# A hand-listed order for attention through inducing points and a SwiGLU network on one core, listed anew

## The chip, the cores and the metric

One core of a Trainium2 chip runs the whole program. The metric is device time in microseconds (us), the median of the runs shown. TensorE (PE in the profile), VectorE (DVE), ScalarE (ACT) and GpSimd (POOL) each work through their own queue in order and wait for one another by semaphores. SyncE (SP) issues nearly all DMAs. TensorE has two rows in the profile: PE is the matmuls, PEld the loads of stationary weights ahead of them.

## What is computed

Four batches of 12416 rows with 128 channels go through two attention steps (32 learned rows look at the input, then the input looks at the 32 rows that come out), and every row of the result goes through a gated network of 1536 hidden channels behind an RMS norm.

```python
def mab(q, kv):                      # B, N, C = 4, 12416, 128; inducing has 32 rows
    s = scale * (q @ kv.transpose(0, 2, 1))
    s = s - s.max(-1, keepdims=True)
    a = np.exp(s)
    a /= a.sum(-1, keepdims=True) + 1e-09
    return a @ kv
h = mab(I, x)
x = mab(x, h)
...
xn = x / np.sqrt(np.mean(x * x, axis=-1, keepdims=True) + 1e-06) * rms_g
g = xn @ w_gate                      # 128 -> 1536
silu = g * (1.0 / (1.0 + np.exp(-g)))
out = silu * (xn @ w_val) @ w_out    # 1536 -> 128
```

## The kernel before

**Tiling.** The rows of a batch are cut into 25 units: 20 of 512 columns, 4 of 480 and one of 256. A unit meets the 1536 hidden channels in 12 chunks of 128, so the network has 4 x 25 x 12 = 1200 blocks. Attention's second step is folded into the gate and value weights (the stacks "sg" and "sv"), so a block starts from the attention weights "a" of its unit.

**A block.** It takes a gate product (`gate`, L656) on TensorE, its SiLU on ScalarE (`silu`, L666), a value product on TensorE (`value`, L684) and their product on VectorE (`times_value`, L698). The way from there to the output is one of three kinds, a letter for each block in the string `sorts`:

- P, plain: one matmul with 32-bit weights (`project_plain`; it appears at L754 with the weight "wo", as two records).
- S, split: a rounded upper half on ScalarE (`high`, L711), the rest on VectorE (`low`, L717), two matmuls with rounded weights (`project_two`, L742 and L743), the sum of both halves on GpSimd (`add_in_place`, L762), and a third matmul (`project_third`, also L754, with weights from "xn" or "more").
- D, split as well: the upper half on ScalarE (`high`, L708), the rest on GpSimd (`low_of_u`, L724), one more step on ScalarE (`high_down`, L730), and then as S from `project_two` on.

So an S block costs VectorE one step more than P, GpSimd one, ScalarE one, and TensorE three short matmuls in place of the plain one. A D block costs GpSimd two steps and ScalarE two more than P.

**The end of a unit.** `scale_up` (L786, ScalarE), `finish` (L795, VectorE), `turn_out` (L801, VectorE) and `store` (L814, four DMAs).

**Attention for the next batch** runs among the blocks of the one before: 1132 small steps ("micros"), among them loads (L100, L111), transposes of the input (L301), scores (L318), sums (L370), and for each set of units a chain that makes the norm (L523 to L582). `gather` (L594) copies the result of that chain into the tile "a" of a unit by four DMAs.

**The order.** Up to the first gate product the order is a list of names (`ORDER`). Everything behind it is a string: `program` (L1257) has a letter for each step, "." being the next of the micros, whose number is in `taken` (L1361). The steps are issued in the order of the letters, and since every engine runs its queue in order, the string fixes the order on all engines and on SP's DMA queue. Six more strings go with it: `banks` (L1141) names the PSUM bank, of eight, that each matmul group writes, `workers` (L1168), `outputs` and `holders` (L1175) name buffers in SBUF, `sorts` (L1198) has the kinds, and `picks` (L1211) says which of the blocks that are ready a step takes. A matmul into a bank waits until the last reader of what the bank held before is done; for a gate product's bank that is `silu`, for a value product's bank `times_value` or, with S blocks, `low`.

```python
do = {"g": gate, "s": silu, "y": lambda: silu(True), "x": gate_times, "v": value, "m": times_value, "h": high, "l": low,
      "n": low_of_u, "e": high_down, "q": project_two, "d": add_in_place,
      "r": project_third, "p": project_plain, "E": scale_up, "F": finish, "T": turn_out, "O": store, "a": lambda: gather(*next(gathered))}
for name in "".join(program.split()):
    if name == ".":
        step, args = micros[int(next(taken))]
        step(*args)
    else:
        do[name]()
```

Of the kernel before, what the change touches and what calls it, by code (L numbers as in the profile page):

```python
# [23 lines left out]
def kernel(  # L24
# [1100 lines left out]
    def seams():  # L1125
# [16 lines left out]
        0234567120374516023741053614753614753641734617543671543613565436125461234512351364127153421432415304251034521342  # L1142
        1546243612631246347631475236423426407234673427637542374532052315034150432015245371453741037637167351675062701231
        7517017374534130142042301270432174126436741562174327156714506134614561056035462013663276261651762307157643054603
        1405364051342605341643625672174251670517614057427645705460760370274261462347347634627475617543206750135401657154
        7014605726415240657465364025423743043045012751350537056175017136731653725702170516751745246754275271263417345325
        0123102431042106524623603240546037426340731037610371057615763516370535610357413713527412534127302503243410145125
        6154572450125062012576173563057037143603607360246327407207320734263121450214352142451320461204321323131435714357
        1437513265615063105607157105612703106302610427640736273073042562364235463253462536712467126512613025710270175012
        7524317157050375136753675021706730267216471601707310434065314015341207534203524054736423450475425432501432605302  # L1150
        5430653654703570367046502305623072567506706427015460754067046274342350473543521727403430724323023607245032706547
        3476451473514354603710375073451230175017450742741765024175641327561432764126701452040674517453172651621140716472
        1046245204314212654205670251704510470274257347320545364510631643156043516045613401642063064732634732630124317461
# [12 lines left out]
        250647356270536257
    """
    workers = """  # L1168
        2102102121021021020210120201010101021021021021212120201200202202020210210210210201201201212120120120120120120120
# [6 lines left out]
        abcdefghicdafjklmgnohbecfpqrslmnahjkidgboelpnqfchmrglsfnobahgpcejfhgeqlnkmbhgsripqojldenagmkhisblfrcpgohedibsjdn  # L1176
        laqmfbrkgpiceabfonlrgpqhicmsekodnjlgfimrepsqnhcbedlikgoahcbmjkprliemqbfdohsrnckgpeamjnqibkcfsldoghpmrjfkesldhain
        obkfgrcsilpmjgqenrokbgscqfmhdailjnpqrmseldohjfncbiaqkmgeprslaejobimsgdqlnpfhjarcdomekqnbjgeraodmkepjclqirsmnpkfa
        oehlrqmsjniogldscpbrkojlhqfaepsnrgmokdblipcaesqgjnhmbpflhrosqckapjefrldiongmscpqdmrefkblgaojdhpasefonqmcjrlkhgsf
        ibqmodehbclnjpkrqiasgcflmakrjeasobhpqgkjcndlifgbhasncokjgerlapmiqodscjfbkrpagqnjishblmpoqknjregadilfmspcqhgbonfk  # L1180
        liqjhmpsrofklcnqgoehjmabisdgfrkphcnjqalomgbreihcpsflbnjdaqohrkipsmngdiljeafmprcgqnksobefdgmhpraeloigfjqknbdchmps
        lfeokrbamhnicjdpoagrqeinjcskagbmleprodfgenqijpchfbgomnicrjaldesgbqpohledbfankdrmsljcgqoeabprhignqeksmpdrjlcgahfk
        obsndmpriehgaqdkjlfosrnmbliqpfgcdfikrdlomsjqapnikerfbljophgcdaikrbnmqhoifcpkandbosmprqeglainkfjehobcmprgfnqlsmho
        irafjpnkmcldsoemfbgnlqkihjgmcebradipnjmqlshfkrdcepboqagsjfhdalkcomnpfirhgbeqsjacfbcnlijqekoacrspmhbgdfkpaichrbok
        mnslegfjhdaqpmofskeircdljmgaqhbnsafklepmoqrinksoajlfpqrnmdcbghieksrofamjhcipnrgdobaqleprmhnodjkgfapceniabsjdmkqo
        lrnbephcgmifkdqplenoamrfschljgqbkimedafhrnsgmfqchbpdeljromnhkqbfpaiscgbmrneiklqdfsoghcijqsbkglphcinmajocfrsdejha
        lpiocdkbeqngrsoedkimlfjbpghadcqnrohkemisldfgpchbjqkahminsfelrbghdkjonasmfbglqpockrndaefjihglkbcpasrhneodqmlfghjn
        bqipkaomcflsgeahdjfrolcbqnmigefjsrahdgpojqklmghfdrncpseokbmjidaehrqfcgbidmaojkrhpneqfslcgekbpimnshqlocrdaspqfjkm
        hagebosmerajdqinhfckmlpojbfsrngcdqlkeimhnpacogbfimqsdhbkfronjplragmcheqgisbarkdmnojfqchigplersmaqdcnpgojhflrksqb
        gimnhfpqalcdmborjkgspnaoheigjmqrfbeloscpindehakjmsgpncbidfmkgsqjreloapihcfmbkjdegflrpahsonkcdimleqpshjonbcrgekns  # L1190
        dqmaflbriphcgjekonsladfpcbqjrgldbpeankfsqicobfrpalminsehgcodbirqgjlcfmkeongprcdajbilfmqhsopnegihrmldqcafkpjnshgo
        qekrbisacgomjpfqlngshdbfjeiqconalksgjpqdebrohalcqfimkedjnslirhdqpcjomkansriqbmgfelhdpjakqmcfraldkonqipsmhgkelcbf
        gipjrmdlnahqibkgpcleosajdbfrqlpjmahrikodgcjselnprbagckjdflqionmpsrhgebidkjcsonrlfdmghaqbkpiesocnkdjplrimqcfehasb
        ojgniclamrqdhpnksmfrlbohjkcmqspeiabfgordlnjcmhegdialbnsjqkmfdhpicoegjrhcfglhnoapgkqesjmlarcdfebpkrsigncdbmlqpofj
        naehrkbmqdljpocaerbmishlegfpnoqmdjkslcrahoipgjebqchforsipnjafmbgqdlekohcgfsrjqlihdekmopabsjcrdlnaoecigkmsocjqprk
        fljhbmpqcskgqhomlarsnq
    """
    sorts = """  # L1198
        PPPPPPPPDPDPPSPPPPPPSSSSDSPSPSSPDSDPPPPDPDPPDSSSPDDSSPDSPSDSSSDPDPPPDPSDPSPPSDSPPDDSPPSPDSSDSSSSSDSPSDSSDSSSPSSS
        SDDPSSPSSPSPSPSDSSSPSSSSSSPSDPSSSDSSSDSSPSSSSSSPDSSSSPSSDSPSSSPSSPPSSSSDSSSSSSSSSSSDSPSSDSDSSSSDPSSSSDSPPSSPPSSD  # L1200
        SSPSSPDSSPSPSSSPSDPPPSDSSSPSSPSSSDDPPSPSSPDPDSSPPSSPSPSPSSSPSSSPSSSSSDSDSSSSPSDSPSSSDDPSSSPSPDSSDSPPSPSPPSSDDSPP
        SPPPDDDSDSPDSPSSPDSSSPDSPDSSPSSPDPDPDPDPSDSSSPDPSPSDSPPSPDSSDSDSPSSDPSSSDSPSDSPPDPPDSSSSSSSSSSSSPPPPSSDSPSSDSSDS
        PSSPDSSSSDSDSSSDSPPSPSSPSSSSSSDSSSPSDPSSSSSPSSPSSSDSDSSSPSDSDSPDSPPPDSDPPSSSSSSPSPSDSSSSPSSSSPSSSPSDSPPSPSDSSSSD
        PSSSPPDDSPPDSSSPSPSPSSSPSPSSPSPPSSDSSSDSSPSSSPSDDDSSPPSSSSDPSPSSSPSDPPSDPSDSDPPPSDSSDPDPDSPSPSPSPDSDSSDSDSPPPDSD
        PPSPPSDSDPSSPDSPSSDSPSDSDPPSSDPSSDSSSSSPSDSPDSPSSSPSPPSSPSSPSSSSDDPPPDSSSSDSSSSSPDSSSSDSSSSSPSSSPSDPDSSSSPSPSSSS
        SSSSSDSSSPSSPDSSSSDSSSDPSPSSPPSSSPSPSDSPDSSPSPSSDPSSSDSSPSSPPSDSSSSSPPSSPDSPSDSPPPPDSSSSSSPSPPSPSSDSSPSPSSPSDSSS
        SSSSSSPSSDSDPPPSDSSPDSDPSSPSSSPSSDPSSDSPPSSPSSSSSSSPSPSSPDSSDSSSPSPSSDSSSSSSSPSSPPSSPSPSSPDSSSSSSDSPSPSSSSPSDSSS
        PDSPSDPDSSPSPSPSSSSSSPSSPSSSSSSSDSSSPPSSSDSDSSSSPSSPSDSPDPSSPSPSSPSSSSSPSSDSSPDSSPSSSPSSSSSDPSSDSPPSSPSDSSSPPSSP
# [242 lines left out]
```

## Time and profile before

| what | us |
|---|---|
| median of 3 runs | 1502.71 (1502.44 to 1503.11) |
| the profiled execution's own time | 1502.65 |
| its span in the trace | 1500.9 |
| TensorE busy (matmuls) | 1487.7 |
| VectorE busy | 1454.2 |
| GpSimd busy | 1420.1 |
| ScalarE busy | 1325.7 |
| first gate product | 48.3 after the span's start |

The profiled execution's time is 0.06 us under the median, so sums made against it hold for the median as well. "Busy" is the time in which at least one instruction of the engine is on record. On VectorE, ScalarE and TensorE the next instruction starts before the record of the last one ends, so what an instruction costs its engine in a full queue is the distance between two starts, and not the duration of one.

### The profile page before, as it was taken

The page shows a single profiled execution, that of the slowest core. Times are in us where ns is not written, and L with a number is a line of the kernel's source. Part 1 is how long each engine was busy: PE and PEld are TensorE (multiplying, and loading weights), DVE is VectorE, ACT ScalarE, POOL GpSimd, SP SyncE. Part 2 cuts the span into 40 slices and gives each one's busy share as a digit, 9 for nine tenths or more (in the row PEclk, how much of TensorE's full clock was granted, in tenths as well). Part 3 has the DMA queues.
Part 4 walks back from the last instruction along what each step waited for, and adds up shares of the span by engine and source line. Part 5 has one row for each costly group of instructions (what it writes and reads, how often), then busy time and mean ns, then how long its engine had stood idle before and what let it go on. Part 6 is the DMA issues. An engine that isn't in the chain of part 4 may idle for free.

```text
span 1500.9 us, 25969 instructions
## 1 busy us (share of the span) xinstructions
PE 1487.7 (99%) x7197; PEld 1101.3 (73%) x7197; DVE 1454.2 (97%) x2575; ACT 1325.7 (88%) x2743; POOL 1420.1 (95%) x1346
## 2 busy tenths in 40 slices
PE   8999999999999999999999999999999999999998
PEld 6557677776776777776787677777678777777776
DVE  6999999999999999999999999999999999999998
ACT  5899899898988889888899888989899989899986
POOL 1499999999999999999999999999999999999998
PEclk9999999999999999999999999999999999999999
DMA  7475425436572213545656222264122112222222
GB/s 284 98 113 91 95 38 108 104 83 87 84 119 45 49 35 67 113 106 102 106 102 96 43 42 40 49 130 112 27 52 39 32 37 42 36 40 39 41 37 41
DMA packets 389329, 112.56 MB, mean 75 GB/s; under 512 B 365088, under 2 KB 369728, under 8 KB 386624
## 3 DMA queue, kind: packets, MB, share of 16 engines
q1 hardware_dynamic: 388592, 110.83, 38.5%
q8 instruction: 57, 0.93, 0.3%
q14 instruction: 88, 0.72, 0.2%
q10 hardware_dynamic: 592, 0.08, 0.0%
HBM read 53.95 MB, written 27.00 MB: 54 GB/s over the span
## 4 chain that ended last, share of the span: by engine, by line
PE 91%; DVE 3%; POOL 2%; ACT 2%; issue 1%; DMA 1%; SPq 0%; DVEq 0%; ACTq 0%; POOLq 0%
PE gv L754 29%; PE gv L684 16%; PE gv L656 16%; PE gv L742 12%; PE gv L743 11%; PE gv L318 3%; PE gv L527 1%; POOL u L762 1%; PE gv L370 1%; POOL xn L762 1%; DVE gv L698 1%; PE gv L855 1%; ACT silu L666 1%; DMA xn<-in_x_dram 1%; DVE xn L717 0%
## 5 line engine op out<-in xcount | busy, mean ns | idle before, releaser
L666 ACT ACTIVATE silu<-gv 128x512 f32<-128x512 f32 (+2 forms) x1193 | 681.4, 590 | 88.6 <-PE gv L656 65.4
L656 PE MATMUL gv<-a,sg 128*128 128x512 f32 (+2 forms) x1188 | 503.7, 424 | 1.2 <-ACT silu L666 0.7
L684 PE MATMUL gv<-a,sv 128*128 128x512 f32 (+2 forms) x1188 | 464.3, 413 | 0.3 <-ACT o L786 0.3
L698 DVE TENSOR_TENSOR gv<-silu,gv 128x512 f32<-128x512 f32 (+2 forms) x684 | 447.3, 668 | 8.9 <-PE gv L684 4.2
L762 POOL TENSOR_TENSOR u<-xn,u 128x512 fp32r<-128x512 f32 (+2 forms) x308 | 379.8, 1244 | 3.4 <-PE gv L743 2.3
L762 POOL TENSOR_TENSOR xn<-xn,xn 128x512 fp32r<-128x512 f32 (+2 forms) x300 | 374.2, 1257 | 5.1 <-PE gv L743 4.8
L711 ACT ACTIVATE xn<-gv 128x512 fp32r<-128x512 f32 (+2 forms) x587 | 339.3, 586 | 28.4 <-DVE gv L698 18.9
L698 DVE TENSOR_TENSOR u<-silu,gv 128x512 f32<-128x512 f32 (+1 forms) x509 | 332.8, 666 | 6.9 <-PE gv L684 2.6
L754 PE MATMUL gv<-u,wo 128*128 128x512 f32 (+2 forms) x650 | 324.5, 585 | 0.2 <-DVE u L698 0.2
L656 PEld LDWEIGHTS gv<-a,sg 128*128 128x128 f32 x1188 | 224.2, 189 | 106.3 <-issue 23.2
L684 PEld LDWEIGHTS gv<-a,sv 128*128 128x128 f32 x1188 | 223.8, 189 | 96.5 <-ACT silu L666 15.7
L717 DVE SCALAR_TENSOR_TENSOR xn<-xn,gv 128x512 fp32r<-128x512 f32 (+2 forms) x346 | 226.0, 658 | 5.2 <-ACT xn L711 2.7
L762 POOL TENSOR_TENSOR xn<-xn 128x512 fp32r<-128x512 f32 (+2 forms) x149 | 184.2, 1242 | 4.5 <-PE gv L743 3.7
L717 DVE SCALAR_TENSOR_TENSOR u<-xn,gv 128x512 fp32r<-128x512 f32 (+2 forms) x241 | 156.1, 653 | 1.8 <-ACT xn L711 0.7
L742 PE MATMUL gv<-xn,xn 128*128 128x512 f32 (+2 forms) x389 | 150.7, 388 | 0.0
L762 POOL TENSOR_TENSOR u<-u 128x512 fp32r<-128x512 f32 (+2 forms) x118 | 147.3, 1252 | 0.9 <-PE gv L743 0.7
L754 PEld LDWEIGHTS gv<-u,wo 128*128 128x128 f32 x650 | 120.7, 190 | 28.6 <-issue 11.4
L742 PE MATMUL gv<-xn,more 128*128 128x512 f32 (+2 forms) x343 | 134.9, 393 | 0.0
L724 POOL TENSOR_TENSOR xn<-u,xn 128x512 fp32r<-128x512 f32 (+2 forms) x103 | 129.9, 1263 | 4.0 <-ACT xn L708 3.6
L730 ACT ACTIVATE xn<-xn 128x512 fp32r<-128x512 f32 (+2 forms) x170 | 106.0, 627 | 5.4 <-POOL u L724 2.9
L708 ACT ACTIVATE xn<-u 128x512 fp32r<-128x512 f32 (+2 forms) x170 | 105.9, 626 | 1.6 <-DVE u L698 0.9
L754 PE MATMUL gv<-u,xn 128*128 128x512 f32 (+2 forms) x240 | 91.4, 387 | 0.0
(215 smaller groups left out, 2371.0 us busy)
## 6 DMA issues: line engine op xcount, KB each, us to landing
out_dram<-o SPq DMA_DIRECT2D x320, 64.0 KB, 2.0
xT<-in_x_dram SPq DMA_DIRECT2D x60, 256.0 KB, 5.3
xn<-in_x_dram SPq DMA_DIRECT2D x60, 256.0 KB, 5.7
a<-hi SPq DMA_DIRECT2D x156, 64.0 KB, 2.0
a<-lo SPq DMA_DIRECT2D x156, 64.0 KB, 2.0
xn<-in_x_dram SPq DMA_DIRECT2D x5, 1024.0 KB, 9.7
xn<-w SPq DMA_DIRECT2D x18, 256.0 KB, 3.9
out_dram<-o SPq DMA_DIRECT2D x64, 60.0 KB, 2.0
```

Source lines behind the costliest of these rows:

```text
L656: nc.tensor.matmul(g[:, 0:T], stacks[b][0][:, ts(j, P)], halves_in_turn(one["a"][:, 0:T]), start=True, stop=True)
L666: nc.scalar.activation(sl[:, 0:T], gates.pop(n)[:, 0:T], AF.Silu)
L684: nc.tensor.matmul(v[:, 0:T], stacks[b][1][:, ts(j, P)], halves_in_turn(one["a"][:, 0:T]), start=True, stop=True)
L698: nc.vector.tensor_tensor(out=to, in0=sl[:, 0:T], in1=v[:, 0:T], op=ALU.mult)
L711: nc.scalar.activation(hi, t["u"], AF.Copy, scale=-(1.0 - 2.0 ** -13) * 2.0 ** -12)
L717: nc.vector.scalar_tensor_tensor(out=t["lo"], in0=t["hi"].bitcast(F32), scalar=4096.0, in1=t["u"], op0=ALU.mult, op1=ALU.add)
L724: nc.gpsimd.tensor_tensor(out=t["lo"], in0=t["u"], in1=t["hi"].bitcast(F32), op=ALU.subtract)
L730: nc.scalar.activation(t["hi"], t["hi"].bitcast(F32), AF.Copy, scale=-(2.0 ** -12))
L742: nc.tensor.matmul(to, weight_of(0, j), halves_in_turn(t["hi"]), start=not one["q"], stop=False)
L743: nc.tensor.matmul(to, weight_of(1, j), halves_in_turn(t["lo"]), start=False, stop=last)
L754: nc.tensor.matmul(to.rearrange("p (n h) -> p h n", h=2) if step2 else to, lhsT, rhs, start=one["left"] == NJ, stop=one["left"] == 1)
L762: nc.gpsimd.tensor_tensor(out=t["lo"], in0=t["hi"].bitcast(F32), in1=t["lo"].bitcast(F32), op=ALU.add)
```

## The change

All strings but `outputs` are replaced: the steps behind the first gate product are listed in another order, with other banks, buffers and kinds. The functions and the instructions that a step issues stay as they are. The same 1132 micros, 1200 gates and values, 100 stores and 97 gathers are issued. Counting the letters of `sorts` gives 325 P, 688 S and 187 D before and 354 P, 661 S and 185 D after; by batch, P goes from 88, 82, 80 and 75 to 97, 89, 84 and 84. `program` has 11323 letters before and 11205 after, 118 fewer, which are the steps that the 29 blocks no longer take.

```diff
@@ -1139,266 +1139,263 @@
     banks = """
-        0234567120374516023741053614753614753641734617543671543613565436125461234512351364127153421432415304251034521342
...
+        7012345627045173420715435407365470634575673056475634705345637506471504653047503461741751347312471532417527134524
...
     """
     workers = """
-        2102102121021021020210120201010101021021021021212120201200202202020210210210210201201201212120120120120120120120
+        2102102102102102011201021210101010120120120120202021201200202202020120120120120102101201212120120120120120120120
         120
     """
     holders = """
-        abcdefghicdafjklmgnohbecfpqrslmnahjkidgboelpnqfchmrglsfnobahgpcejfhgeqlnkmbhgsripqojldenagmkhisblfrcpgohedibsjdn
...
+        abcdefghiefdcjklmbahgidnopqrscbfjekahgrdifcgilnbgompsficgdrqbhjlfgomdpknibhsrjeofagcbnldphiqksmjobdrecaigqsfkpab
...
     """
     sorts = """
-        PPPPPPPPDPDPPSPPPPPPSSSSDSPSPSSPDSDPPPPDPDPPDSSSPDDSSPDSPSDSSSDPDPPPDPSDPSPPSDSPPDDSPPSPDSSDSSSSSDSPSDSSDSSSPSSS
-        SDDPSSPSSPSPSPSDSSSPSSSSSSPSDPSSSDSSSDSSPSSSSSSPDSSSSPSSDSPSSSPSSPPSSSSDSSSSSSSSSSSDSPSSDSDSSSSDPSSSSDSPPSSPPSSD
...
-        SSPSDSSSPSSPSDSSPSSSSPDSSSSSPDSSPSSDPSSDPSSPPPSPSSPSDPPSPDSSSPPSSSPSSSSSSSPSSSSS
+        PPPPPPPPPPDPPSPPPPPPSSSSDSPSPSPPDSDPPPPDPDPPDSSPDSDSSPDSPSDSSSDPDPPPDPSDPSPSPDSPPDDSPPSPDSSDSSSSSPSDSDSSDSPSPSSS
+        SDDPSSSPSPSSSPPPSDSPSSSSSSPSDPSSSDSSSDSSPSSSSSSPDSSSSPSSDSPSSSPSSPPSSSSDSSSSPPSSSSSDSPSSDSDSPSSDSSSSSDSPPSSPDSSP
...
+        SSSDPSSSPSSPSDSPSSSSSPDSSPSPPDSSPSSDPSSDPSSPPPSPSSPSDPPSPDSSSPPSSSPSSSDSPSSPSSPP
     """
     picks = """
-        CCACCCAAABBAAABBAAAAABBAAAABAABAABBAAABBAAAAADAAAAAAABAABAAADAABAACBBBABBBABAAAAAAAABABAAAAABACBAAABBBBBABBBAACA
...
+        EEDCBABAAABBAABAAABAAABAAAAAAAAAAAAADADABAAAAAABABAADCABCBABCABAAAAABABAAAAACAAAAAAAAAACBAAACBBAABAAAAAABBAAAAAA
...
     """
     program = """
-        ........ggs.vvs.vgmgs.vg.m.vgsm.s.mmvg..v.g.p.s.p...s.pms.g.sm.v..gp.s...pm..gps..v.v..pm.mgps....vgv.mv.gsmg.pm
-        h......gv..ph.v.s.psmsgvm..hm.g..nps.sgnlv.gpem.eqvs.qsvmdgEvgmsaqmg.svrvmsgvm.vspdm...hpmhdlph..h.vlg.psl..gmr.
...
-        ghqslpdmvgqmplhdElvhgrmsvgdqlhqmsrglsvqhpmdslTdghqvsglvOdvqmgvmqsdvmrhgmpsdlhmsdqlrhrvdlqhrmrrdlhqrFrrdqrlrTdqrp
-        EOdrrrrrFTO
+        ...g..vvg.vsgg...sm.svmsgmgv.svm.sm.gg.v.spm...vmsp.......p.g..ggsp...m.p.sp.....vs.vv..gv.p...m.gp.m.svmgsgm.v.
+        s.mhmvp..v.s.gp..s.p.h..g..g..sm.glp..ngsg.p.mev.vsqmp.mvsv.Evgsmgp.m..vsm.vsggm..v.pmsph.m.hlvsdplhghmv.glsg.rl
...
+        dmvvqsmvhqmdrmphlhvlnrgFhqghlpsTdsregEOvmrqdslqmqvvghgpmdssvmdglrgmvsvrqhmpshdmrlqdlhgqrlspdFqrdrvqTrpdEmrOrpdpr
+        rrFTO
     """
     taken = """
-        5 0 9 80 54 1 41 55 81 2 3 56 110 57 42 43 109 11 10 6 17 12 44 7 108 13 45 18 19 4 14 114 46 25 15 47 21 59 107
...
+        9 41 0 5 10 1 54 2 80 3 55 42 110 6 4 7 43 109 44 108 45 11 17 12 25 13 46 14 19 15 114 18 47 56 21 20 33 107 27
...
     """
```

More of the change, by code (lines that the diff above doesn't have):

```diff
@@ new lines @@
+        5264302641035463426145613474215674157456702140145143041754371035103754201420527052375470752074561740651274721075
+        0171072305167320563061376021621715467501750736507630627502307230567320513670215602745270256741564051620104256042
+        4364230247652475325463124735245231572020362031652301316021065210635761275612756745162574577134572137142307120317
+        4201372013407647536153575617317514046176154271542162146746751257132517372053172501753054234012731624074107264172
+        4615401265372350265350237536247320470367206137263175012375610256315042560236504203547364032652425402561402675072
@@ new lines @@
+        5475643562456427534273460532406534525205635701623652036123762147324302746024635270427427405702145721507253045103
+        4324312460320631034263245312567417324157371631765317053127061742036471274130275021340571247316724531654312360123
+        4653362173650367103106751047653475634534753042603541354167356734137456374635610543175612463172631476162314573217
+        5350432503274507520475213721074063476343072130360130612356021356135706517601526561520642054250426014627067060560
+        4305674305742564230625436254214265421053612051260510642462167120713023074103141536415746741356234726573257324754
@@ new lines @@
+        7204357046524350435421352045134107213475214531245261231653206530452064573407142145271520764512742107410516230456
+        1364531645317625372167261372065712357523156243417534613705140614063465461206342603426706173026370653053652326027
+        3651717610512741675417412542152674275430572031513715327130627365132501201750734573456150315630307213041704610316
+        3405134765164203172037261026357135605173251754735265465732675263206376130761320716307671276371537165341635643576
+        4351642345234605260231062546231603507521067150647251726527652175217361573206152065123561230124045102470621407256
@@ new lines @@
+        3072136713671561231547236436013071027323615732607367531746251475216457216512041705172502730216732016325012702757
+        1540173524154103170261062416724140651746216047216376134176421743125741620574150761507615634017536573415364576257
+        0417265176503215707015735272540251320341420642603213024156246345634646145647134675316257247327213203423074167712
+        3013206275306536723603472407520470417207521075102652467546127152761523157264361351653761756717031607356045160576
+        1464576145715723451631256712515670125712561420672416247123467132763741023602461026712017475471502472342143254275
@@ new lines @@
+        sjqorhmfcgpqkiedrcgnpombedlshqrjkfgaocnhbiqapmjeokldcnsjrpbfglhcioefpcgbmjnspdlrgkqpfhcnmaksgpdbfqojaehgnkimlrbe
+        cihqpnfsjodgkhraqpenmigekocbfrsljhniqadbcfenphfkogljmqrieahdsnbkmfelcahrqjkifgasohlpjbmeidrcfalginkqmishdpoeljqr
+        mnksfapiobglmchedakngfqrcjplisoghkacbmqfgcelndhbmjrpsgifkoclnahedbqsirpckmgfeaojbidrlpqcgnhfoksrjlbmpceaifnghcbo
+        mdjlknpqbehasrfigbojcklnpqhdgecsfadgrmeknpldisqcojbarmhgkfdnbsaepidoqrlnhcbkmoesgfdacrqbjpgsnlkofcihdgmjeprsaihq
+        dcebonlmkspgacjrbihfabokclpqjfsmrnoeblagqidhscfbprmogeknlpqdgaembjifqdghlroaesknjfqpcaolmfescrnbgmhdaqsepjomifbk
@@ new lines @@
+        qecrlgienodfphmrsagjkilpbcndgmrejsofqlbhageiqnomcbdlrhajkifgdsqpncalbiopjgfindsmrqkeahclrnsdimajblforqghkpmincje
+        sohqmlbrnifdakjcgaseplhqosigdfkrampbjnlsqkocegdjihlfaonbhmpsqrkgcdjhebrodalnegfbmpskdqricbmoefgalpsnjdakqrhelmsp
+        jraokensfpiglcqbodheagmjnprfaqoikslrgdcbhienmagplqbefjrokdnsmgaqeichdmqbfjcinrphgledgaosmkilgdnbqjfaropsecqnfelb
+        armihcjpgaskdfoqinreldgmsfkibjhblacnrmdgbpjfceosqnmrbhdkpgilofahsjcgbkieqlhncdqfgspabmelrkojqghnmiadslbcejpfqrad
+        kjoigbhcslapqekdfrjncomprkfgbenjasqcklophmidenbcrmsaqoghkidlncrjpkqefbsdcoilnmgqprsfjmahoklqebgcfarjoimfeglpkqrh
@@ new lines @@
+        abnsodmilcafkbpreqlnjsmgihafeknsofcpdqrjmklbhgaiqfnepgbcshdrqkojfnlebmsacdijrnkfaepmloqsbhcgfanjrleokncigbfepmqd
+        jhsrfolknqeaicpolmjgsbkrcnhjdlsmfaickjnraqpiomdlhegbakscdnjliaeogbqrmnhcfkpojdaslbqmcgohernkjafqipdscbgoemrplnhs
+        fabdkoqnscdegmpfadiqebrsljghkmfenqpadcrboiglsnqohfdkipcejrmlagdsnbfjqdkbohpeiamcrglsnjqodfkrmpnhedqglobcimjsndae
+        cflhsboeiknmqpdlarocisjphflmgbesjrkagnpocsqlbfoianrdgpcljekmsfhadoleqsjpbhanidkqogrmfnjcekadgsolqbfhprmnkjiachdb
+        glspqeihfmrkcdlanepohjmlbpqokgaisnrldejcofhkbipqgsjradioehmnklbgpcfsqrjhpbgmadsficknqolpegdhimrjcbqkolahsngpmodj
@@ L1256 @@
+        ACAABBCABABAADBAADAAACBBBBAABAAAACABABAAAAABAAAAAAAABAAAAAAABAAAACBAAAAAEAABAAAADAACBAABAABBAAAACAACABCAABAAAAAA
+        AAABAAABAAABDCABAAABAAABBBABBAAAAAABAAACBBABBAAAAAAAAACABAABABAABBAAABBA
     """
     program = """
[L1258 to L1260 removed]
```

346 lines of the change are left out of this document (153 added, 193 removed), and 70 rows, old and new, of the table taken.

## The prediction

> **What bounds the kernel now.** I read the page's busy line first, then its chain of waits.
>
> ```profile
> span 1500.9 us, 25969 instructions
> PE 1487.7 (99%) x7197; PEld 1101.3 (73%) x7197; DVE 1454.2 (97%) x2575; ACT 1325.7 (88%) x2743; POOL 1420.1 (95%) x1346
> PE 91%; DVE 3%; POOL 2%; ACT 2%; issue 1%; DMA 1%; SPq 0%; DVEq 0%; ACTq 0%; POOLq 0%
> PE gv L754 29%; PE gv L684 16%; PE gv L656 16%; PE gv L742 12%; PE gv L743 11%; PE gv L318 3%; PE gv L527 1%; POOL u L762 1%; PE gv L370 1%; POOL xn L762 1%; DVE gv L698 1%; PE gv L855 1%; ACT silu L666 1%; DMA xn<-in_x_dram 1%; DVE xn L717 0%
> ```
>
> The chain runs through TensorE for 91% of the span, but three engines are nearly full. The stretches of 50 us show how nearly; the last row sums all thirty.
>
> ```profile
> 0.00:50.00 50.00, 44.55 (x473) 32.30 (x474) 35.81 (x104) 28.35 (x61) 10.28 (x20) 1.00 0.63 230
> 600.00:650.00 50.00, 49.88 (x378) 38.73 (x377) 48.28 (x83) 43.92 (x91) 48.98 (x45) 1.00 0.56 117
> 1300.00:1350.00 50.00, 50.00 (x210) 38.84 (x210) 49.92 (x84) 44.95 (x91) 49.97 (x45) 1.00 0.15 29
> sum 1500.00, PE 1487.67 PEld 1101.27 DVE 1454.17 ACT 1325.68 POOL 1420.13; mean PE 49.59 PEld 36.71 DVE 48.47 ACT 44.19 POOL 47.34
> ```
>
> The columns after the window are PE, PEld, DVE, ACT and POOL. Behind the first 50 us VectorE is busy for 1454.2 - 35.8 = 1418.4 of 1450.9 us and GpSimd for 1420.1 - 10.3 = 1409.8. In the last batch (row 1300) neither has a tenth of a us free; in the middle (row 600) they have 1.7 and 1.0. TensorE's busy time is modelled, so I count its passes instead, with the distance between starts in the timeline.
>
> ```profile
> 1300.71 0.38 PE L743 MATMUL gv<-xn,more 128*128 128x512 f32 x1
> ...
> 1302.44 0.38 PE L742 MATMUL gv<-u,more 128*128 128x512 f32 x1
> ...
> 1304.75 1.29 DVE L698 TENSOR_TENSOR gv<-silu,gv 128x512 f32<-128x512 f32 x2
> ...
> 1305.72 1.08 ACT L711 ACTIVATE xn<-gv 128x512 fp32r<-128x512 f32 x2
> ...
> 1309.99 1.02 PE L754 MATMUL gv<-u,wo 128*128 128x512 f32 x2
> 1310.05 2.53 POOL L762 TENSOR_TENSOR xn<-xn,xn 128x512 fp32r<-128x512 f32 x2
> ...
> 1310.44 0.78 PE L684 MATMUL gv<-a,sv 128*128 128x512 f32 x1
> ...
> 1311.06 1.02 PE L754 MATMUL gv<-u,wo 128*128 128x512 f32 x2
> ```
>
> From 1300.71 to 1302.44 lie eight starts of passes: 0.216 us each. From 1309.99 to 1311.06 lie one plain matmul and one pass: 1.07 - 0.216 = 0.85, or four passes. In a full queue a VectorE step takes about 0.60 (1.29 for two, less 0.69 for one), GpSimd 1.24, ScalarE 0.48. With the widths of the units a mean step is 0.97 of these. The blocks need 2 x 1200 + 3 x 875 + 4 x 325 = 6325 passes of 0.2095 us: 1325 us. From the first gate product (48.3) to the end are 1452.6, so 127 are left for attention's matmuls and for idle time.
>
> ```profile
> L318 PE MATMUL gv<-xT,hT 128*32 128x512 f32 (+2 forms) x192 | 27.4, 588 | 0.2 <-ACT silu L666 0.2
> L527 PE MATMUL gv<-eT,gram 128*128 128x512 f32 (+2 forms) x54 | 26.1, 564 | 0.1
> L318 PE MATMUL gv<-xT,indT 128*32 128x512 f32 (+2 forms) x224 | 25.8, 546 | 0.2 <-ACT xT L861 0.2
> L370 PE MATMUL gv<-xn,e 128*32 128x128 f32 x570 | 17.6, 274 | 0.0
> ```
>
> These take up to 97 us, so TensorE idles for at least some 30 of 1452.6, about as much as VectorE (32) and GpSimd (41). The idle time is where the new order can gain: all three are at 97 to 98%.
>
> **What TensorE's idle time is.** Two views of one place, loads first, then matmuls, and the waits of the loads (us in total, times, longest):
>
> ```profile
> 702.45 0.19 PEld L684 LDWEIGHTS gv<-a,sv 128*128 128x128 f32 x1 [0.24 <-DVE xn L717]
> ```
> ```profile
> 702.24 0.38 PE L656 MATMUL gv<-a,sg 128*128 128x512 f32 x1
> 702.45 0.48 PE L684 MATMUL gv<-a,sv 128*128 128x512 f32 x1
> 702.77 0.38 PE L754 MATMUL gv<-u,more 128*128 128x512 f32 x1
> ```
> ```profile
> PEld gv L656 <- ACT silu L666: 16.7, 60, 1.1
> PEld gv L684 <- ACT silu L666: 15.7, 64, 0.5
> PEld gv L656 <- DVE u L698: 7.7, 27, 0.8
> PEld gv L684 <- DVE u L698: 7.0, 25, 0.8
> PEld gv L656 <- DVE xn L717: 6.6, 24, 0.8
> PEld gv L684 <- DVE xn L717: 6.1, 18, 0.8
> PEld gv L754 <- POOL u L762: 5.3, 18, 0.8
> PEld gv L754 <- POOL xn L762: 5.0, 15, 0.8
> ```
>
> A load normally runs under the pass before it. Here it was held until the matmul's own turn, and the next matmul came 0.32 later in place of 0.216: a held load costs TensorE 0.10. These rows have 251 held loads, so they cost up to 25 us; behind a plain matmul of 0.85 a held load costs nothing, so I take 20. The Trainium skill, TensorE: Matmul & The Clock Gate, section LDWEIGHTS, gives a load as its columns over 1.2 ns, 107 ns for 128. The trace's record of a load is 0.19 and what it adds is 0.10; by the page the 251 would be 27 us.
>
> **The change part by part.** Every sum is made against 1502.65.
>
> Kinds: 29 blocks become plain. TensorE: 29 x (4 - 3) x 0.2095 = **+6.1**. VectorE loses 27 steps of 0.58, 15.7 us. GpSimd loses 27 + 2 x 2 = 31 of 1.20, 37.3. ScalarE loses 27 + 4 = 31 of about 0.47, 14.5. What these are worth depends on the order, so they enter through the next part only.
>
> The order: I cut both listings at every twelfth gate product and added up each engine's work per piece with the intervals above (attention's micros by the rows of their lines, the same in both). A piece takes no less than its busiest engine. Summed over the pieces and averaged over the twelve ways of starting the cut, the busiest engine has 1449.7 us before (measured: 1452.6) and 1444.8 after: **-4.9**, TensorE's 6.1 included, so the evening-out is worth 11.0. With pieces of six it is 1475.7 to 1468.8 (-6.9), with thirty 1433.9 to 1432.5 (-1.4). Twelve comes nearest to the measured time, so I take it. Bounds: +6.1 if only TensorE's work counts, and -6.9.
>
> Held loads: the pieces know nothing of them. Measured in TensorE work listed in between, everything that follows TensorE has moved about one pass away: gate to SiLU has its lower quartile at 0.86 for 0.65, value to product 1.08 for 0.86, `project_two` to its sum 1.51 for 1.29. What precedes TensorE moved nearer: VectorE's last read of a bank to the next matmul into it has its median at 0.86 for 1.08, the GpSimd sum to the third matmul 2.16 for 2.37 at the quartile. That is the picture of TensorE's steps listed at the start of their load, one pass ahead of the matmul. A listing of that kind keeps the shortest distances: the one in fifty for a bank that VectorE frees is 0.20, where the old one's 0.22 less a pass is nothing. But most distances are shifted, not longer, and most held loads name a bank (silu, u L698, xn L717). I take **-3.0** between 0 and -20, near the small end for that.
>
> The longer distances behind TensorE also meet these waits:
>
> ```profile
> ACT silu L666 <- PE gv L656: 65.4, 159, 1.4
> POOL xn L762 <- PE gv L743: 8.5, 19, 1.5
> ```
>
> ScalarE is busy for 88%, so its 65.4 us cost nothing now; if they went, nothing would follow. GpSimd's 8.5 lie within the evening-out.
>
> SP's queue: gathers, stores and loads move among one another. A gather's four DMAs must land before the unit's first gate product.
>
> ```profile
> DMA to landing us min/median/max: 1.8/2.0/6.4
>   PE gv L656: 0.4, 1
> ```
>
> That is the view of `gather`: one wait, 0.4 us. The shortest listed distance from a gather to its gate product is 3.59 us of TensorE work before and 3.64 after. I cost the move at 0; TensorE's own work hides it, and if that were gone, 6.4 - 3.6 = 2.8 per late gather. Gathers with a load of the input listed shortly ahead and a distance below 4.3 are four before and two after. The end: both lists close with two third matmuls, `finish`, `turn_out` and the store, 0.
>
> Sum: 1502.65 - 4.9 - 3.0 = 1494.75, **1494.8 us**.
>
> **The rivals.**
>
> *TensorE pays and the others only idle.* Place: the 29 added plain matmuls, 20 of them in batches 0 to 2, where VectorE and GpSimd have idle time already; they finish still earlier and wait. It decides as soon as evening-out and held loads together give less than 6.1. The time is 1502.65 + 6.1 = 1508.8. For it: PE has 91% of the chain, and row 1300 has VectorE and GpSimd both full at once while of 149 additions on GpSimd (the row of L762 below: fastest, median, slowest in ns) the slowest took 1713 and the median 1279, in a span where VectorE was nearly always busy. A rule that takes work from both for a shared port's sake would then take it needlessly.
>
> ```profile
> L762 POOL TENSOR_TENSOR xn<-xn x149: 724/1279/1713, 74.0 to 1494.9; 128x512 fp32r<-128x512 f32 x111, 128x480 fp32r<-128x480 f32 x30, 128x256 fp32r<-128x256 f32 x8
> ```
>
> The Trainium skill, SBUF — State Buffer, section Who interferes with whom, says the same: a VectorE instruction with at most one SBUF input (and outside its two-port modes) doesn't contend with GpSimd, and those of L698 and L717 read one tile in SBUF and one in PSUM; the trace agrees. Against this rival: the pieces.
>
> *A tight order.* Held loads mostly vanish (-14 of 20) with the evening-out: 1502.65 - 4.9 - 14 = 1483.8. For it: row 1300 of the windows shows that all three engines can be full at once. Against it: batches 0 to 2 carry attention's short matmuls.
>
> *It cancels.* Evening-out of 6 against 6.1: 1502.6.
>
> *SP's queue ends late.* Two gathers late by 2.8 on top of the cancelled sum: 1502.6 + 5.6 = 1508.2. Against it: the 0.4 us above, with four such before.
>
> **How the numbers follow.** Forecast 0.46, TensorE pays 0.20, tight 0.16, cancels 0.13, SP's queue 0.05. The forecast's own range is 1488 to 1501. The range to hold 8 in 10 reaches from the tight order's 1484 to the first rival's 1509. A difference under 0.2% (3 us) can't be told from none. Faster by more: nearly all of the forecast and the tight order, 0.61; the same: 0.14; slower: the two slow rivals, 0.25.
>
> **What would show it.** The count of plain records is 708 (650 before). VectorE's busy time falls by about 16 and GpSimd's by 37, so both get more idle time, and TensorE's first idle causes, the held loads of the eight rows, should number fewer than 251. SiLU's wait for the gate product should fall well under 65. If the span is longer with fewer held loads, the first rival holds; if gathers appear among TensorE's waits, the last. I am wrong in the mechanism if TensorE's waits grow while VectorE and GpSimd idle.

## The result, and the profile after

The changed kernel takes 1494.64 us, the median of four runs (1494.50 to 1495.03), beside 1502.91 for the kernel before on the same chip (1502.44 to 1503.32): a ratio of 0.9946 with a 95% interval of 0.9928 to 0.9963. The predicted time was 1494.8.

First the page's span, busy line and chain of waits.

```profile
span 1493.2 us, 25861 instructions
...
PE 1481.1 (99%) x7168; PEld 1106.8 (74%) x7168; DVE 1443.0 (97%) x2548; ACT 1307.9 (88%) x2712; POOL 1388.0 (93%) x1315
...
PE 95%; DVE 3%; ACT 1%; issue 1%; SPq 0%; DMA 0%; POOL 0%; DVEq 0%; ACTq 0%; POOLq 0%
...
L754 PE MATMUL gv<-u,wo 128*128 128x512 f32 (+2 forms) x708 | 350.5, 581 | 1.1 <-DVE u L698 1.1
```

The span is 7.7 us shorter. The plain matmuls number 708, as the kinds say. VectorE's busy time fell by 11.2 and GpSimd's by 32.1, both by more than the span, so both have become emptier; the chain now runs through TensorE for 95% of the span in place of 91%. The stretches of 50 us (PE, PEld, DVE, ACT, POOL behind the window):

```profile
600.00:650.00 50.00, 50.00 (x330) 39.74 (x325) 48.11 (x84) 43.35 (x90) 48.84 (x46) 1.00 0.60 130
1300.00:1350.00 50.00, 50.00 (x210) 38.59 (x209) 49.57 (x84) 45.88 (x94) 48.96 (x45) 1.00 0.20 38
```

In this stretch of the last batch GpSimd has one us free of fifty where it had none, and VectorE 0.4. Two engines idle more while the whole is quicker: the third, TensorE, must idle less. I took that from all matmul records: of each distance between two starts, the part beyond the passes of the first. It sums to 55.1 us before and 42.3 after. Behind the first 50 us it is 42.2 and 29.7, so 12.5 less, and of these 8.5 are gaps of 0.05 to 0.15, whose number fell from 303 to 214: gaps of the size of the prediction's held loads. The account is +6.1 of added work, -12.5 of idle time and -0.6 in the front, ahead of where the two orders part and so not due to the change, -7.0 in all, beside -7.7 in the span; 0.7 stays unassigned. By the start of a numbered gate product the lead is 1.7 at the first, 4.2 at the 200th, 6.4 at the 500th and 8.6 at the 700th, with ups and downs of one or two us between. Behind that it grows no more: 8.1 at the 900th, where the last batch starts, 5.9 at the last one and 7.7 at the end. So these starts show no gain in the last batch, in which all three engines are fullest.

The waits (us in total, times, longest):

```profile
ACT silu L666 <- PE gv L656: 77.3, 163, 2.0
...
PEld gv L656 <- ACT silu L666: 18.6, 63, 0.8
...
POOL xn L762 <- PE gv L743: 14.8, 31, 2.0
PEld gv L684 <- ACT silu L666: 12.9, 46, 0.8
...
PEld gv L684 <- DVE u L698: 7.5, 27, 0.8
...
PEld gv L754 <- POOL xn L762: 4.9, 15, 0.8
...
PEld gv L656 <- DVE u L698: 4.6, 19, 0.5
PEld gv L754 <- POOL u L762: 4.5, 11, 0.8
...
PEld gv L684 <- DVE xn L717: 3.7, 14, 0.6
...
PEld gv L656 <- DVE xn L717: 3.1, 10, 0.8
```

The eight rows of loads fell from 251 waits to 205. Over all rows of the block steps the loads whose idle time ends with a named releaser fell from 485 to 368, while those that wait for nothing the profile names rose from 354 to 407. Against that ScalarE waits longer for the gate product (77.3 for 65.4) and GpSimd longer for `project_two` (14.8 for 8.5). The waits have moved from TensorE to engines that had become emptier. The view of `gather`:

```profile
who waited for it (us, times):
busy tenths in 40 slices 0000000000000000000000000000000000000000
DMA to landing us min/median/max: 1.8/2.0/8.8
```

Nobody waits for a gather, though the slowest lands after 8.8 us (6.4 before).

### The profile page after: what moved, and what is told of

Read it like the earlier page. It is cut to its first block, busy times and chain, and to the rows that moved or that the text cites. A ratio compares the mean times of both kernels' runs of the same rounds, so it can differ in the third digit from the quotient of the medians.

```text
span 1493.2 us, 25861 instructions
## 1 busy us (share of the span) xinstructions
PE 1481.1 (99%) x7168; PEld 1106.8 (74%) x7168; DVE 1443.0 (97%) x2548; ACT 1307.9 (88%) x2712; POOL 1388.0 (93%) x1315
## 4 chain that ended last, share of the span: by engine, by line
PE 95%; DVE 3%; ACT 1%; issue 1%; SPq 0%; DMA 0%; POOL 0%; DVEq 0%; ACTq 0%; POOLq 0%
PE gv L754 31%; PE gv L656 17%; PE gv L684 17%; PE gv L742 12%; PE gv L743 12%; PE gv L318 3%; PE gv L527 1%; PE gv L370 1%; PE gv L855 1%; DVE u L698 0%; DVE we L250 0%; PE gv L464 0%; PE gv L154 0%; DMA out_dram<-o 0%; SPq L814 0%
## 5 line engine op out<-in xcount | busy, mean ns | idle before, releaser
L666 ACT ACTIVATE silu<-gv 128x512 f32<-128x512 f32 (+2 forms) x1193 | 669.2, 590 | 105.2 <-PE gv L656 77.3
L656 PE MATMUL gv<-a,sg 128*128 128x512 f32 (+2 forms) x1188 | 455.4, 417 | 1.2 <-ACT o L786 0.6
L684 PE MATMUL gv<-a,sv 128*128 128x512 f32 (+2 forms) x1188 | 440.6, 409 | 0.1
L698 DVE TENSOR_TENSOR gv<-silu,gv 128x512 f32<-128x512 f32 (+2 forms) x657 | 426.4, 671 | 6.7 <-ACT silu L666 2.3
L762 POOL TENSOR_TENSOR xn<-xn,xn 128x512 fp32r<-128x512 f32 (+2 forms) x333 | 413.4, 1251 | 11.6 <-PE gv L743 10.0
L698 DVE TENSOR_TENSOR u<-silu,gv 128x512 f32<-128x512 f32 (+2 forms) x536 | 346.8, 663 | 8.6 <-ACT silu L666 2.9
L754 PE MATMUL gv<-u,wo 128*128 128x512 f32 (+2 forms) x708 | 350.5, 581 | 1.1 <-DVE u L698 1.1
L762 POOL TENSOR_TENSOR u<-xn,u 128x512 fp32r<-128x512 f32 (+2 forms) x256 | 315.6, 1243 | 8.6 <-PE gv L743 7.0
L717 DVE SCALAR_TENSOR_TENSOR xn<-xn,gv 128x512 fp32r<-128x512 f32 (+2 forms) x346 | 226.6, 664 | 6.6 <-ACT xn L711 4.6
L762 POOL TENSOR_TENSOR u<-u 128x512 fp32r<-128x512 f32 (+2 forms) x137 | 171.3, 1255 | 1.8 <-PE gv L743 1.2
L762 POOL TENSOR_TENSOR xn<-xn 128x512 fp32r<-128x512 f32 (+2 forms) x120 | 151.4, 1264 | 6.5 <-PE gv L743 4.8
L717 DVE SCALAR_TENSOR_TENSOR u<-xn,gv 128x512 fp32r<-128x512 f32 (+2 forms) x206 | 133.2, 654 | 2.7 <-ACT xn L711 1.4
```

The lines of the kernel that those rows point to most:

```text
L656: nc.tensor.matmul(g[:, 0:T], stacks[b][0][:, ts(j, P)], halves_in_turn(one["a"][:, 0:T]), start=True, stop=True)
L666: nc.scalar.activation(sl[:, 0:T], gates.pop(n)[:, 0:T], AF.Silu)
L684: nc.tensor.matmul(v[:, 0:T], stacks[b][1][:, ts(j, P)], halves_in_turn(one["a"][:, 0:T]), start=True, stop=True)
L698: nc.vector.tensor_tensor(out=to, in0=sl[:, 0:T], in1=v[:, 0:T], op=ALU.mult)
L717: nc.vector.scalar_tensor_tensor(out=t["lo"], in0=t["hi"].bitcast(F32), scalar=4096.0, in1=t["u"], op0=ALU.mult, op1=ALU.add)
L754: nc.tensor.matmul(to.rearrange("p (n h) -> p h n", h=2) if step2 else to, lhsT, rhs, start=one["left"] == NJ, stop=one["left"] == 1)
```

## The experiments

All times are medians; each is compared with the kernel before on the same chip, whose medians lay between 1503.10 and 1503.23. "Idle" is TensorE's idle time counted as above. "Pieces" is what the prediction's sum over pieces of twelve gate products gives for the edit, against the order it was made from. The column "against its own order" sets medians beside each other that were taken beside different medians of the kernel before (1502.91 for the new order), so a few tenths of a us in it mean nothing.

| run | us | ratio to before (95%) | against its own order | pieces | idle |
|---|---|---|---|---|---|
| before | 1502.91 | 1 | | | 55.1 |
| after | 1494.64 | 0.9946 (0.9928 to 0.9963) | -8.3 from before | -4.9 | 42.3 |
| e1, old order with the new number of kinds | 1513.55 | 1.0066 (1.0053 to 1.0078) | +10.4 | -2.0 | 59.9 |
| e2, old order, 29 matmuls less | 1502.68 | 0.9996 (0.9987 to 1.0005) | -0.5 | -1.8 | 61.4 |
| e3, new order, 29 matmuls less | 1492.09 | 0.9922 (0.9909 to 0.9936) | -2.6 | -2.7 | 45.2 |
| e4, old order, VectorE and GpSimd lighter | 1501.81 | 0.9990 (0.9981 to 0.9999) | -1.4 | -7.3 | 53.5 |
| e5, old order, all three lighter | 1499.89 | 0.9980 (0.9971 to 0.9989) | -3.2 | -10.9 | 59.3 |
| e6, new order, VectorE and GpSimd lighter | 1493.81 | 0.9941 (0.9929 to 0.9954) | -0.8 | -4.4 | 41.7 |
| e7, old order, steps moved ahead of held loads | 1510.49 | 1.0048 (1.0035 to 1.0062) | +7.4 | | 63.1 |
| e8, new order, the same | 1497.71 | 0.9964 (0.9952 to 0.9977) | +3.1 | | 45.2 |
| e9, old order, only block ends put back | 1504.27 | 1.0007 (0.9998 to 1.0016) | +1.0 | | 56.4 |
| e10, new order, the same | 1495.45 | 0.9947 (0.9935 to 0.9960) | +0.8 | | 42.1 |
| e11, new order, shorter bank lead | 1528.70 | 1.0169 (1.0155 to 1.0183) | +34.1 | 0 | 75.3 |
| e12, new order, 40 products in SBUF | 1527.75 | 1.0169 (1.0155 to 1.0183) | +33.1 | | 75.0 |

**Kinds without the order (e1).** 29 S blocks of the old order become P where they stand; their steps that P doesn't take drop out, everything else stays in its place. One row of `sorts`:

```diff
-        SDDPSSPSSPSPSPSDSSSPSSSSSSPSDPSSSDSSSDSSPSSSSSSPDSSSSPSSDSPSSSPSSPPSSSSDSSSSSSSSSSSDSPSSDSDSSSSDPSSSSDSPPSSPPSSD
+        SDDPSSPSSPSPSPSDSSSPSSSSSSPSDPSSSDSSSDSSPSSSSSSPDSSSSPSSDSPSSSPSSPPSSSSDSSSSPPSSSSSDSPSSDSDSSSSDPSSSSDSPPSSPPSSD
```

> The old order with 29 of its S blocks made plain in place (9, 7, 4 and 9 by batch; each loses its steps on ScalarE, VectorE and GpSimd, and the two short matmuls; the third becomes the plain one). Theory 'order': the gain of the change is in the order of the queues, and TensorE sets the end; then the 29 plain blocks alone cost their TensorE time less what fewer late operands give back: 1505 to 1509. Rival 'kinds': the gain comes from relieving VectorE (-16 us) and GpSimd (-36 us), whatever the order: 1493 to 1498.

It took 1513.55, more than either theory allowed. The page of e1:

```profile
span 1511.3 us, 25805 instructions
...
PE 1496.4 (99%) x7168; PEld 1099.3 (73%) x7168; DVE 1442.7 (95%) x2546; ACT 1313.4 (87%) x2714; POOL 1387.9 (92%) x1317
```

VectorE and GpSimd are as busy as in the changed kernel to within 0.3 us (1443.0 and 1388.0 there), and TensorE has the same number of matmuls. The work on the engines is that of the new kernel, and the time is 18.9 longer. So this number of kinds doesn't bring the gain by itself; it comes with the new listing. With the old listing, TensorE's work rose by its 6.1 and its idle time by 4.8 besides. Two things were not run: the new listing with the old kinds, and the old listing with exactly the new kinds. The two kernels differ in the kind of 130 blocks, and e1 changes 29, of which 25 are plain in the new kernel too.

**Less work, same order (e2 to e6).** Left out are, for 29 blocks, the third matmul (6.2 us of TensorE, e2 and e3) or, for the same blocks, the addition on GpSimd (36 us) together with 26 of the `turn_out` transposes on VectorE (16 us; e4 and e6), or all of these (e5). The edit of e2 ("..." stands for further block numbers):

```diff
     def project_third():
         n = lists["r"].pop(choices.pop(0))
+        if n in (55, 91, 120, ..., 1096, 1125):
+            unit_of(*blocks[n][:2])["left"] -= 1
+            factor_of.pop(n)
+            return
```

> The old order with the third matmul of 29 split blocks of 512 columns left out (their part of the output is missing), 29 x 0.2155 = 6.2 us less on TensorE and nothing else. If TensorE alone sets the end: 1496.5. If VectorE and GpSimd set it as much (they idle as little): a third of that, 1500 to 1501.

> The same 29 third matmuls left out of the new order. VectorE and GpSimd have more idle time there, so both theories have TensorE set the end: 1494.6 - 6.2 = 1488.4, and 1490 if the other engines' waits take a quarter back.

The old order gave back nothing that can be told from zero for 6.2 us of TensorE: its idle time rose by 6.3. The new order gave back 2.6. Both times lie above all that was expected (1501 at most for e2, 1490 for e3).

> The old order with 29 of GpSimd's additions (36 us) and 26 of VectorE's closing transposes (16 us) left out: those 29 blocks and 26 units come out wrong. TensorE's work stays. This is the relief that the new kinds give, without their price on TensorE and without the new order. Theory 'order': held loads that name a bank stay, 1500 to 1502. Rival 'evening-out': VectorE and GpSimd were two of three bounds, 1493 to 1497.

> The old order with all three reliefs at once: the 29 third matmuls (6.2 us of TensorE), the 29 additions (36 us of GpSimd) and the 26 closing transposes (16 us of VectorE) left out; those blocks and units come out wrong. Theory 'joint bound': no engine alone sets the end, so one relief gave 0 (TensorE) or 1.4 (the other two), and all together give TensorE's 6.2 or more: 1495 to 1497. Rival 'chains': the order itself, by waits from engine to engine and back, sets the time, and all three give little more than the sum of 0 and 1.4: 1500 to 1502.

> The new order with the same 29 additions of GpSimd and 26 closing transposes of VectorE left out. Theory 'joint bound': both have more idle time already, so it gives less than the 1.4 of the old order: 1493.5 to 1494.6. Rival 'chains': the same 1.4 or more, 1491 to 1493.2.

Relief on VectorE and GpSimd was worth 1.4 in the old order, as the theory 'order' has it and not the 'evening-out'. In the new one it was worth 0.8, which lies in the range of the 'joint bound' and not in that of 'chains'; the runs of e6 reach from 1493.47 to 1496.11, so 0.8 can't be told from nothing and doesn't decide between the two. Relief on all three in the old order, by about 6, 16 and 36 us, was worth 3.2: hardly over the edge of what chains of waits would give and well short of a joint bound of the three. The page of e5, and its last batch:

```profile
PE 1485.7 (99%) x7168; PEld 1097.4 (73%) x7168; DVE 1440.5 (96%) x2549; ACT 1324.1 (88%) x2743; POOL 1386.3 (92%) x1317
...
PE 94%; DVE 2%; ACT 1%; DMA 1%; issue 1%; SPq 0%; POOL 0%; DVEq 0%; ACTq 0%; POOLq 0%
```
```profile
1300.00:1350.00 50.00, 50.00 (x209) 38.53 (x208) 49.53 (x84) 44.75 (x91) 48.90 (x44) 1.00 0.18 32
```

The reader should see two things. VectorE and GpSimd have 49.53 and 48.90 in this stretch, almost the new order's 49.57 and 48.96, and the chain has 94% on TensorE, almost the new order's 95%. Yet e5, with less work on all three engines than either kernel, is 5.2 us slower than the new one. Neither the busy row nor the chain's share by engine tells which order is quicker.

**Held loads taken one by one (e7 to e10).** Where the trace showed a held load, a later TensorE step that was ready was listed ahead of it: 183 steps in the old order (e7), 106 in the new one (e8). A row of `program` in e7:

```diff
-        h......gv..ph.v.s.psmsgvm..hm.g..nps.sgnlv.gpem.eqvs.qsvmdgEvgmsaqmg.svrvmsgvm.vspdm...hpmhdlph..h.vlg.psl..gmr.
+        h......gpv..h.v.s.psmsgvm..hm.g..nps.sgnlgv.pem.eqvs.qsvmdgEvgmsaqmg.svrvmsgvm.pvsdm...hpmhdlph..h.vlg.psl..gmr.
```

> The old order with 183 steps on TensorE's queue alone moved ahead by one to three places: wherever the old trace shows a weight load held by a late operand or bank, a later step of that queue whose operands were there goes first. All other queues keep their order, and the work is the same. Theory 'held loads': each costs TensorE 0.1 us and the end follows: 1487 to 1495. Rival 'joint bound': TensorE's time was no bound by itself (6.2 us less of its work gave nothing), so 1500 to 1503.

> The same repair on the new order, 106 steps of TensorE's queue moved ahead of a held load. Theory 'held loads': 1486 to 1491. Rival 'joint bound', with the new order's TensorE worth 0.4 us a us as 6.2 us less of its work showed: 1490 to 1494.5.

Both theories missed: the old order lost 7.4 and the new one 3.1. The waiting loads of the block steps that name a releaser are 485 in e7, the very number of the kernel before; a load that was spared was replaced by another. I took the loss to be because a gate or value product that is put back delays ScalarE and VectorE, and with them the next bank. So I repeated it where only the end of a block is put back, a third or plain matmul, which frees no bank for others in the middle of a block: 63 steps (e9) and 33 (e10).

```diff
-        pd.e.med..sv.E.qhdrmrgh.qsglnrhrgsvlqasdgmvevgmqsdqmhgsvlr.sdvvmgpmhdFsvgrh.m.dhmsqlhgvn.rsg.pElsdmgevqmhgnv.s.q
+        pd.e.med..sv.E.qhdrmrgh.qsglnrrhgsvlqasdgmvevgmqsdqmhgsvlr.sdvvmgpmhdFsvgrh.m.dhmsqlhgvn.rsg.pElsdmgevqmhgnv.s.q
```

> The old order; only where the held load belongs to a third or a plain matmul, with which a block's chain ends, does a later step of TensorE's queue go first: 63 steps moved. Gates, values and the two short matmuls are never put back behind one another's followers. Theory 'chains': putting back a gate, value or pair delays everything behind it, which is why 183 swaps cost 7.4 us; an end can wait, so these 63 cost nothing and give up to 63 x 0.1: 1496.5 to 1502. Rival 'any change to a fitted order costs': 63/183 of 7.4 more, 1504 to 1506.

> The same on the new order, 33 steps. Theory 'chains': 1491 to 1494.6. Rival 'any change to a fitted order costs': 106 swaps cost 3.1, so 1495 to 1496.

Neither moved by as much as 0.1%, and neither gained. Both times lie in the range of the rival 'any change to a fitted order costs' and outside that of 'chains', so the reason I gave for e7's loss is not borne out; +1.0 and +0.8 are too near to the noise to refute it. In none of the four runs could a held load be bought off for 0.10 us by a local exchange.

**Bank lead (e11).** The steps stay as they are; from block 260 on, gate and value product of every fourth block take the bank freed second longest ago in place of the longest, the others the longest. In the listing, the matmuls with less than 0.3 us of TensorE work between the release of their bank and their own turn go from 190 to 320 of 2698. One row of `banks`:

```diff
-        0171072305167320563061376021621715467501750736507630627502307230567320513670215602745270256741564051620104256042
+        0171072305167320563061376021621715467501757063570363270537603756230576125630271062341261320647021470234071234715
```

> The new order, step for step, with other PSUM banks: the gate and the value product of every fourth block take the bank that was freed second longest ago in place of the longest. Listed with less than 0.3 us of TensorE work between a bank's last read and its next matmul are then 320 steps in place of 190. Theory 'late operands and banks': 130 more held loads of 0.1 us each, plus what is handed on, 1503 to 1515. Rival 'held loads are an echo': there is slack elsewhere, 1494 to 1497.

It cost 34.1 us with no instruction added on any engine, well over both ranges: 0.26 for each of the 130 matmuls with a short lead. The busy line of e11, whose counts are those of the changed kernel, and its waits:

```profile
PE 1507.6 (99%) x7168; PEld 1102.2 (72%) x7168; DVE 1453.5 (95%) x2548; ACT 1314.4 (86%) x2712; POOL 1390.0 (91%) x1315
...
ACT silu L666 <- PE gv L656: 100.5, 203, 2.0
...
PEld gv L656 <- ACT silu L666: 28.4, 84, 0.8
PEld gv L684 <- ACT silu L666: 24.7, 76, 0.8
POOL xn L762 <- PE gv L743: 21.1, 45, 1.2
```

A late bank shows twice: the load waits for SiLU, which still reads the bank, and a few steps on SiLU waits for the gate product that was held. All four rows grew at once. As I read it, the ring of gate product, SiLU, bank and next gate product has no slack to take up such a delay. (The 0.26 is an average: with every fourth block's banks changed, longer leads shifted as well.)

**The port (e12).** 40 S blocks keep their product in a free buffer in SBUF in place of the PSUM bank, by a letter that `times_value` treats as it treats P and D; banks were given out anew by longest free (169 leads under 0.3, so no shorter than in the new order). VectorE's `low` then reads two SBUF tiles.

```diff
-        SDDPSSSPSPSSSPPPSDSPSSSSSSPSDPSSSDSSSDSSPSSSSSSPDSSSSPSSDSPSSSPSSPPSSSSDSSSSPPSSSSSDSPSSDSDSPSSDSSSSSDSPPSSPDSSP
+        SDDPSSSPSPSSUPPPSDSPSSSSSSPSDPSSUDSSSDSSPUSSSSSPDSSSSPSSDSPSSSPSUPPSSSSDUSSSPPSUSSSDSPSSDSDSPSSDSUSSSDSPPSSPDSSP
```

> The new order, step for step; 40 S blocks put their product into a free SBUF buffer and not back into the value's PSUM bank, so the bank is free at the product and not 2.8 us later at `low`, and the banks are given out anew, longest free first (steps with less than 0.3 us of lead: 169 for 190). `low` of these blocks then reads two tiles in SBUF. Theory 'banks': at the price of the last run (34 us for 130 short leads) 21 fewer give 5 us, 1489 to 1494. Rival 'port': each of the 40 steps on VectorE meets a GpSimd addition (1.24 us, GpSimd is busy for 93%) and takes about 1.3 in place of 0.68, 25 us more on VectorE, some of it handed on: 1500 to 1520.

It took 33.1 us more, beyond both ranges. The steps of L717 and of L762 in e12, and last one row of each in the new order (ns: fastest, median, slowest):

```profile
L717 DVE SCALAR_TENSOR_TENSOR xn<-xn,gv x320: 380/674/692, 71.4 to 1517.2; 128x512 fp32r<-128x512 f32 x127, 128x480 fp32r<-128x480 f32 x28, 128x256 fp32r<-128x256 f32 x5
...
L717 DVE SCALAR_TENSOR_TENSOR xn<-xn,u x26: 694/1246/2226, 151.5 to 1423.7; 128x512 fp32r<-128x512 f32 x26
L717 DVE SCALAR_TENSOR_TENSOR u<-xn,u x8: 1053/1352/1524, 544.6 to 1449.3; 128x512 fp32r<-128x512 f32 x8
L717 DVE SCALAR_TENSOR_TENSOR u<-u x6: 692/876/1736, 239.3 to 1440.7; 128x512 fp32r<-128x512 f32 x6
```
```profile
L762 POOL TENSOR_TENSOR xn<-xn x120: 731/1282/1808, 80.6 to 1518.4; 128x512 fp32r<-128x512 f32 x99, 128x480 fp32r<-128x480 f32 x19, 128x256 fp32r<-128x256 f32 x2
```
```profile
L717 DVE SCALAR_TENSOR_TENSOR xn<-xn,gv x346: 380/680/690, 70.9 to 1484.4; 128x512 fp32r<-128x512 f32 x141, 128x480 fp32r<-128x480 f32 x28, 128x256 fp32r<-128x256 f32 x4
```
```profile
L762 POOL TENSOR_TENSOR xn<-xn x120: 740/1282/1324, 80.1 to 1485.7; 128x512 fp32r<-128x512 f32 x99, 128x480 fp32r<-128x480 f32 x19, 128x256 fp32r<-128x256 f32 x2
```

A step with one operand in PSUM ("gv") never took over 0.69; with both in SBUF the 40 steps took 50.6 us in sum, where 40 x 0.674 = 27.0 were due. That is 24 us of VectorE, and an addition on GpSimd took up to 1.81 where the new order's slowest of the same group took 1.32. How much of the 33.1 is due to this is not shown: the banks differ from the new order's as well, and no run gave them out anew without the 40 steps.

## Why the prediction was right, point by point

**What bounds the kernel.** The prediction had three engines that are nearly full at once. They were full, but in the old order their fullness was not the bound. Work taken from TensorE alone (e2) gave 0.5 us, from VectorE and GpSimd together (e4) 1.4, from all three (e5) 3.2. What the time did depend on, in the new order, is the way through the eight banks: e11 leaves every engine's work alone and costs 34. That the old order was held by the same ring is argued from this and not shown.

**Kinds.** TensorE's +6.1 holds: 708 plain records and, in e1, the same number of matmuls as the new order. For VectorE and GpSimd the 15.7 and 37.3 compare with 14.5 and 37.6 in the sum of all durations; the busy times fell less, by 11.2 and 32.1, so the overlap of records shrank by 3.3 and 5.5. In the old listing these are worth next to nothing by themselves: e4's relief on both engines gave 1.4, and e1, which has the kinds whole, loses 10.4.

**The order, -4.9.** This is the step that failed, though the sum came out. "A piece takes no less than its busiest engine" is a floor; I read its change as a price, on the ground that with twelve gate products the floor comes near to the measured time. The table shows how far it is from one: -2.0 where +10.4 was measured (e1), -10.9 where it was -3.2 (e5), -7.3 where it was -1.4 (e4), 0 where it was +34.1 (e11). Only e3 agrees, and e2 (-1.8) within its interval. That a sum of maxima comes near the whole time did not give it the right slope here.

**Held loads, -3.0.** The sign and the size were in the bounds: 46 fewer in the eight rows at 0.10 would be 4.6, and with the other rows of the block steps the number fell from 485 to 368. But the split "evening-out 11, held loads 3" is not in the trace. Of the 12.5 of TensorE's idle time that went, 8.5 went from gaps of a held load's size, where this term had 3.0. As I read it, the two terms were one thing counted in two ways, 14.0 together for 12.5 measured. That the total, 1494.75, meets the measured 1494.64 so nearly is therefore luck. Nor is 0.10 a price of its own: the local exchanges (e7 to e10) recovered none of it.

**SP's queue, 0.** Right: no engine waits for a gather.

**What would show it.** The records, VectorE's and GpSimd's idle time and the number of held loads came as said. SiLU's wait did not fall "well under 65"; it rose to 77.3. ScalarE has 17.8 us less to do, and so stands waiting earlier: e1, where it has 12.3 less in the old order, has 77.9 in the same row and is the slower kernel. By the prediction's own words that wait lies beside the path, so its fall should not have been named as a sign.

**The rivals.** "TensorE pays" is out by 14 us as a whole, but it is what the old order does, worse than priced: 1502.65 + 6.1 = 1508.8, and e1 took 1513.55. Its argument on the port is borne out as a fact of these kernels: neither order gives VectorE two SBUF inputs in its block steps, and their slowest `low` takes 0.69. The Trainium skill, SBUF — State Buffer, section Who interferes with whom, says that a VectorE instruction with at most one SBUF input, outside the two-port modes, doesn't contend with GpSimd, and that one with two SBUF inputs contends with a GpSimd instruction that reads SBUF. The 0.69 agree with the first half, and e12's 40 steps, with a mean of 50.6 / 40 = 1.27, with the second. The tight order wanted 14 us of held loads gone along with the evening-out; the whole fall of idle time was 12.5. "It cancels" and the late gathers fall with the time and with the empty view of `gather`.

**What stays open.** Which property of the new listing makes TensorE idle less was not isolated. It is not a longer lead on the banks: the listing has more leads under 0.3 us than the old one (190 for 93) and idles less. The two orders differ in other ways too (by the trace, behind the first 50 us, a gate product directly follows another 249 times, once before), and no run tried these.

No run beat the new order with the whole computation in it.

## What to carry to other kernels

When several engines of a hand-listed kernel are all at 97%, take work away from one of them and look: if next to nothing comes back, as in the old order here, look for the bound in waits between the engines. In this case neither a sum of loads nor the chain's share by engine priced an edit. Fewer steps dropped into an order listed for more can lose time (here 10.4 us), so search kinds and order together. Keep the bank's lead as a quantity of its own in such a search, and keep one operand of VectorE's steps in PSUM where GpSimd runs beside it.

## What the runs showed of the hardware

- A VectorE step of 128x512 with two SBUF inputs took a median of 1.25 us in its largest group (up to 2.23) beside a GpSimd that is busy for 92% of the span, and 0.67 with one of them in PSUM; GpSimd's additions stretched from 1.28 to as much as 1.81. In the changed kernel itself VectorE's steps of L250 near the start read two SBUF tiles as well. One of the nine ran wholly beside GpSimd steps and took 1.63 us; the other eight, with next to no GpSimd work beside them, took 0.68 to 0.82. Seven of the eight and the slow one are in these rows:

```profile
L250 DVE SCALAR_TENSOR_TENSOR we<-sc,we x6: 677/686/707, 17.2 to 65.5; 128x512 int32<-128x512 int32 x6
L250 DVE SCALAR_TENSOR_TENSOR we<-sg,we x2: 822/1226/1630, 47.8 to 68.6; 128x512 int32<-128x512 int32 x2
```

- 130 more matmuls whose bank was freed less than 0.3 us of listed work ahead went with 34.1 us (e11), 0.26 each on average and more than twice the 0.10 by which one held load delays TensorE. Longer leads shifted in that run too, so 0.26 is no price of one such matmul.
- TensorE work is nearly free to remove in one order (6.2 us for 0.5) and worth 0.4 us for each us in another (2.6), at the same 99% busy.
